# Attention and token/channel mixer on one core: batch 1's scores unpadded over 64 rows in two bursts, batch 0's output product by thirds of the weight

## The chip, the cores and the metric

The kernel runs on one core of a Trainium2 chip. The metric is the device time of one execution in microseconds (us). The kernel before was timed three times: 288.08, 288.24 and 288.31 us, median 288.24 us. The profile comes from a further execution of its own.

## The reference

Two parts follow each other. The first is windowed attention in 8 batches of 8 heads, 576 positions, head size 64: heads 0 to 3 see the last 32 positions ("plain"), heads 4 to 7 see every fourth of the last 128 ("dilated"). The second is a mixer over tokens, then over channels.

```
scores = scale * np.matmul(q, k.transpose(0, 1, 3, 2))          # scale = 1/8
mask_plain = (rel >= 0) & (rel < 32)                            # rel = query - key
mask_dil = (rel >= 0) & (rel < 128) & (rel % 4 == 0)
attn = softmax(np.where(mask, scores, -1e9)); x = attn @ v      # x: (8, 576, 512)
h = np.maximum(xt @ w_tok1, 0.0) @ w_tok2                       # 576 -> 256 -> 576
u = x + h.transpose(0, 2, 1)
h2 = np.maximum(u @ w_ch1, 0.0) @ w_ch2                         # 512 -> 1536 -> 512
return u + h2
```

## The kernel before, in words

**Stages.** A prelude does batch 0's attention and token mixing. Then one stage runs for each batch b. Its main part is `gen_main(b)`, the channel mixer: twelve products `gp` of four matmuls of 512 columns (L768), each with a relu into `gt`, then the output product `yp` (L787) for four blocks s of 128 tokens, 24 matmuls of 256 columns each, with u added by VectorE (L797) and a store. An odd batch carries the last 64 tokens of itself and of the batch before it (`gp_tails` L759, `yp` L807). A block of `gp` with mb from 8 to 11 reads the third piece of w_ch1 (`w_2` in the order, loaded at L860). The output product reads w_ch2 in three pieces of four mb each, loaded by the three DMAs at L988.

**What is woven in.** Between the matmuls of stage b stand steps for later batches: for batch b+1 the values `av` (L601 to L613), token mixing `h1p` (L625, L627), `up` (L637 to L650) giving u, and its transposes `tpu` (L664 to L675) giving `uT`; for batch b+2 casts of q, k and v to 16 bits, transposes `tp_q`, `tp_k`, `tp_t`, and scores. The function `interleave` merges the main part with lists of (time, cost, step), the times written by hand at the end of the file. It decides only the order in which the program is written; each engine then works strictly in that order and waits by semaphores. In the first stage (b = 0) both batch 1's scores and batch 2's are worked on, since the pipeline is filling.

**Scores.** Batches 0 and 1 use `scores_plain` and `scores_dil`: q lies padded with zeros over 128 rows (`qz`), and each score matmul (L425) is preceded by a "veil" (L423), a matmul of the identity with a table that puts −60000 where a key isn't seen. For a head pair that is, with veils, 12 matmuls of 160 columns, 4 of 128 and 8 of 64 if plain, 16 of 128 and 8 of 64 if dilated. After the veil no mask is needed. From batch 2 on (`twinned`) a burst `scores_twin(b, g)` does four heads at once (g = 0 plain, g = 1 dilated): the two heads of a pair use 64 rows each of TensorE, side by side (L510), 24 matmuls a burst, without veils. ScalarE takes the exponentials (L534) in the order of the last small pieces first for batch 2, and GpSimd multiplies by a 0/1 band afterwards (L112, on `attp`, `attt`, `attd`).

**Banks.** PSUM has three groups of banks: main (3, for gp and yp), sc (2) and fl (3, for transposes, av, h1p, up, tpu and part of a burst). A burst takes six banks: for batch 2 in the order fl, fl, sc, sc, fl, main. Who next wants a bank waits for its last reader.

**Queues.** Loads of q, k, v and the stores go out on SyncE's queue (SP); weights and many casts go through GpSimd (POOL). `gate` (L856) is a 1x1 copy on POOL that holds the loads of batch 2 back until the first piece of w_ch2 has landed. POOL's instructions stand in program order, so whatever waits there holds what is behind it.

Of the kernel before, what the change touches and what calls it, by code (L numbers as in the profile page):

```python
# [9 lines left out]
FP16 = mybir.dt.float16  # L10
FP32 = mybir.dt.float32
# [57 lines left out]
def kernel(  # L69
# [275 lines left out]
    def twinned(b):  # L345
        return b >= 2

# [150 lines left out]
    def scores_twin(b, g):  # L498

        tags = (("sc", 2), ("sc", 2), ("fl", 3), ("fl", 3), ("fl", 3), ("main", 3))  # L500
        if b == 2:
            tags = tags[2:4] + tags[0:2] + tags[4:6]
        ps = [bank(*tags[i], f"sc_{b}_{g}_{i}") for i in range(6)]
        small = ps[4:6]

        def twin(hp, banks, c, keys, queries):
            for h in range(2):
                rows = slice(64 * h, 64 * h + 64)
                n = c.stop - c.start
                nc.tensor.matmul(out=banks[h][:, c], lhsT=keys(rows), rhs=queries(rows), start=True, stop=True)  # L510

# [54 lines left out]

        def mask_tails():
            t = attt[:, 2 * g:2 * g + 2].rearrange("p a h c -> p (a h) c")[:, :, 64:TW].rearrange(
                "p z (x c) -> p z x c", c=128)[:, :, :, 0:64]
            mult(nc.gpsimd, t, t, tails_seen[g])  # L570

        yield from small_exps(1)
        if b == 2:
            yield from small_exps(0)
        for hp in (2 * g, 2 * g + 1):
            for h in range(2):
                main(hp, h)
                if h and (g or b == 2):
                    mask(hp)
                    if b == 2 and hp % 2 == 0:  # L580
                        mask_tails()
                yield 0.0
        if b > 2:
            yield from small_exps(0)
            if g == 0:
                mask(0)
            mask_tails()
            if g == 0:
                mask(1)
# [138 lines left out]

    def mix_steps(b, t_h1, t_h1b, t_u, t_uT, du=1.0, turn=6.0, gap=2.6):
        h1 = [sb.tile([128, DM], FP16, tag="h1", bufs=4, name=f"h1_{b}_{jb}") for jb in range(2)]  # L730
# [11 lines left out]
        else:  # L742
            for i, cb in enumerate(CBS):
                steps.append((t_uT + 0.9 * i, 0.28, lambda cb=cb: emit_uT(b, cb)))
        return steps

    def gen_main(b):
# [17 lines left out]
        for mb in range(NMB):  # L765
            p = bank("main", 3, f"gp_{b}_{mb}")
            for i, cb in enumerate(order):
                nc.tensor.matmul(out=p, lhsT=w3_block(cb, mb), rhs=uT[(b, cb)][0], start=(i == 0), stop=(i == 3))  # L768
                if i == 1:
                    yield 0.43  # L770
            relu(nc.vector if (mb % 2 == 1 if b == 0 else mb % 4 != 3 if b == 1 else mb in (1, 5)) else nc.scalar, gta[:, mb, m0:m0 + 512], p)
            yield 0.43
# [82 lines left out]
    def gate(t, src):  # L855
        nc.gpsimd.tensor_copy(out=t, in_=src)  # L856
# [127 lines left out]
    load_w3(2)  # L984
    for i in (2, 3, 4, 5, 7, 6, 8, 9, 10, 11):
# [5 lines left out]
    for cast in casts1[12:]:  # L991
        cast()

    new_qk(2)
    gate(l32[(2, "t")][0:1, 0, 0:1], w4[0][0:1, 0:1])
    for nm in ("q", "k"):
        load_tail(2, nm, nc.sync)
    for h0 in (0, 4):
        for nm in ("q", "k"):
            load_qk(2, nm, h0, h0 + 4, nc.sync)  # L1000
    load_v(2)

# [3 lines left out]
    for b in range(B):  # L1006
        steps = []
        if b == 0:
            steps += score_steps(1, 0, 0, (0.0, 0.7, 1.5),
                                 ((3.0, 5.2), (4.4, 7.0), (7.2, 9.6), (8.6, 11.4)))  # L1010
            va = value_steps(1, 13.4, 0.7)
            steps += va[:4] + [(p + 0.3, c, f) for p, c, f in va[4:]]
# [5 lines left out]
            steps += [(t, 0.25, f) for t, f in zip((25.2, 25.9, 27.0, 27.6, 28.2, 34.8, 35.2, 35.6, 36.0), bare)]  # L1018
            steps += scores2[:10]
            steps += at(34.0, 0.0, [lambda: emit_loads_qk(3)])  # L1020
        elif b == 1:
            va = value_steps(2, 0.0, 1.0)
            steps += [(0.8 + 0.4 * i, c, f) for i, (_, c, f) in enumerate(scores2[10:])]
            steps += [(t, c, f) for t, (_, c, f) in zip((2.2, 3.0, 4.8, 5.6, 8.2, 9.0, 10.4, 11.2), va)]
            steps += mix_steps(2, 7.0, 12.4, 14.6, 24.4, 1.0, 5.6, 0.8)
            casts = cast_steps(3)
            steps += [(6.0 + 0.5 * i, 0.0, casts[i]) for i in (0, 2, 4, 6, 8)]
            steps += [(9.5 + 1.0 * i, 0.0, lambda i=i: cast_qk(3, "q", i, nc.scalar)) for i in range(4)]
            steps += at(11.0, 0.3, casts[9:])
            steps += score_steps(3, 21.0, 4.6, lag=0.1)  # L1030
            steps += at(6.0, 0.0, [lambda: load_v(3)]) + at(20.8, 0.9, load_steps(4))
            steps += at(11.0, 0.9, dma_steps(3)) + at(17.0, 0.4, place_steps(3))
        else:
# [39 lines left out]
```

## Time and profile before

| | |
|---|---|
| median of three runs | 288.24 us |
| profiled execution, its own time | 289.66 us |
| its span in the trace | 287.8 us |
| TensorE (PE) busy in the span | 276.8 us |
| VectorE (DVE), ScalarE (ACT), GpSimd (POOL) busy | 132.1, 134.0, 163.0 us |
| first gp matmul of batch 0, first yp of batch 0 | 28.47, 50.38 us after the span's start |
| first gp matmul of batch 1, of batch 2 | 69.24, 105.06 us |

The profiled execution's own time is 1.86 us above its span (start and end outside the trace), and 1.42 us above the median of the other runs. A row of the timeline has the start in us, the duration in us, the engine, the line, the operation and "output<-inputs". A matmul's duration includes its way through the array; matmuls behind each other start closer together than they last, so the pitch, the distance of starts, is what one costs. A row of the windows view gives an interval, its length and each engine's busy time in it.

### The profile page before, as it was taken

How to read it: one execution, taken by the hardware profiler on the slowest of the kernel's cores; microseconds unless marked ns; L12 is line 12 of the kernel's file. 1: busy time of each engine (PE TensorE's matmuls, PEld its weight loads, DVE VectorE, ACT ScalarE, POOL GpSimd, SP SyncE). 2: the span in 40 equal slices, each digit the busy share in tenths (PEclk: the TensorE clock that was granted, in tenths of full speed). 3: DMA queues.
4: the chain of work that ended last, by engine and by line, in shares of the span. 5: the costliest groups of instructions: out<-in, count | busy, mean ns of one | idle time of the engine just before them, and what ended most of it. 6: DMA issues, size and time to landing. Idle time of an engine off the chain costs nothing.

```text
span 287.8 us, 6995 instructions
## 1 busy us (share of the span) xinstructions
PE 276.8 (96%) x2838; PEld 210.9 (73%) x2838; DVE 132.1 (46%) x278; ACT 134.0 (47%) x265; POOL 163.0 (57%) x221
## 2 busy tenths in 40 slices
PE   5879999999999999999999999999999999999995
PEld 2777676888766886698776976797766966886594
DVE  7747658446764236414640164416440274421022
ACT  2854673263543804574447615482546534225500
POOL 6961860478865799449970999279952930000000
PEclk9999999999999999999999999999999999999999
DMA  7999999993999998979888978299974210431023
GB/s 218 263 211 218 283 225 207 320 218 82 328 210 192 264 264 230 139 164 350 226 159 182 330 224 186 57 219 329 193 150 95 85 64 2 91 112 37 0 76 108
DMA packets 105551, 52.63 MB, mean 183 GB/s; under 512 B 73872, under 2 KB 104464, under 8 KB 105520
## 3 DMA queue, kind: packets, MB, share of 16 engines
q1 hardware_dynamic: 101280, 47.07, 67.0%
q0 software_dynamic: 2640, 3.94, 8.0%
q10 hardware_dynamic: 1600, 1.18, 1.4%
q8 instruction: 22, 0.36, 0.6%
q14 instruction: 9, 0.07, 0.1%
HBM read 37.07 MB, written 9.44 MB: 162 GB/s over the span
## 4 chain that ended last, share of the span: by engine, by line
PE 80%; DMA 8%; DVE 3%; POOL 3%; issue 2%; ACT 2%; ACTq 1%; SPq 0%; POOLq 0%; DVEq 0%
PE yp L787 29%; PE gp L768 24%; DMA l_vd<-in_v_dram 4%; PE h1p L627 4%; PE yp L807 3%; DMA l_k<-in_k_dram 3%; PE up L639 3%; PE sc L510 3%; PE gt L759 3%; DVE xn L112 1%; DMA kr<-c_k 1%; PE h1p L625 1%; PE av L608 1%; PE up L650 1%; PE av L603 1%
## 5 line engine op out<-in xcount | busy, mean ns | idle before, releaser
L787 PE MATMUL yp<-w,gt 128*128 128x256 f16 x756 | 87.1, 273 | 0.0
L787 PEld LDWEIGHTS <-gt 128*128 128x128 f16 x768 | 78.6, 106 | 6.5
L106 ACT ACTIVATE gt<-gp 128x512 f16<-128x512 f32 x69 | 41.2, 597 | 76.3 <-PE gp L768 76.0
L768 PE MATMUL gp<-utd,w 128*128 128x512 f16 x144 | 54.7, 380 | 0.0
L768 PE MATMUL gp<-utm,w 128*128 128x512 f16 x144 | 54.6, 379 | 0.0
L768 PEld LDWEIGHTS <-w 128*128 128x128 f16 x384 | 39.2, 114 | 20.3 <-issue 0.5
L797 DVE TENSOR_TENSOR o<-yp,u 128x512 f32<-128x512 f32 x31 | 21.4, 691 | 63.1 <-PE yp L787 58.5
L112 POOL TENSOR_TENSOR attp<-attp,const 128x1280 f16<-128x1280 f16 x12 | 31.4, 2616 | 27.5 <-ACT attp L534 27.4
L112 DVE TENSOR_TENSOR xn<-av,rec 128x320 f16<-128x320 f32 x64 | 31.4, 491 | 2.2
L112 POOL TENSOR_TENSOR attd<-attd,const 128x1024 f16<-128x1024 f16 x12 | 25.3, 2132 | 1.6 <-ACT attd L534 1.6
L768 PE MATMUL gp<-uT,w 128*128 128x512 f16 x96 | 25.8, 379 | 0.0
L108 DVE TENSOR_SCALAR gt<-gp 128x512 f16<-128x512 f32 x27 | 18.5, 686 | 13.6 <-PE gp L768 13.1
L645 DVE TENSOR_TENSOR u<-up,xn 128x512 f16<-128x512 f32 x26 | 17.9, 690 | 7.5 <-PE up L639 7.5
L534 ACT ACTIVATE attp<-sc 128x480 f16<-128x480 f32 (+1 forms) x36 | 16.1, 536 | 7.4 <-PE sc L510 7.4
L102 POOL CAST c_k<-l_k 128x512 f16<-128x512 f32 x29 | 18.0, 628 | 1.9 <-DMA l_k<-in_k_dram 1.7
L102 POOL CAST c_q<-l_q 128x512 f16<-128x512 f32 x27 | 16.8, 629 | 3.1 <-DMA l_q<-in_q_dram 3.1
L616 DVE RECIPROCAL rec<-av 128x5 f32<-128x5 f32 x64 | 12.2, 190 | 13.8 <-PE av L613 13.7
L106 ACT ACTIVATE h<-h1p 128x256 f16<-128x256 f32 x29 | 11.1, 384 | 14.5 <-PE h1p L627 14.1
L399 POOL COPY kt<-kr 128x512 f16<-128x512 f16 x10 | 10.7, 1075 | 9.0 <-DMA kr<-c_k 9.0
L697 ACT COPY utd<-utm 128x512 f16<-128x512 f16 x12 | 12.8, 1135 | 4.1 <-DMA utm<-u 4.1
L102 POOL CAST vv<-l_vn 128x256 f16<-128x256 f32 x32 | 12.0, 420 | 4.3 <-DMA l_vn<-in_v_dram 4.1
L112 POOL TENSOR_TENSOR attt<-attt,const 128x512 f16<-128x512 f16 x12 | 14.0, 1165 | 0.0
(147 smaller groups left out, 459.9 us busy)
## 6 DMA issues: line engine op xcount, KB each, us to landing
out_dram<-o SPq DMA_DIRECT2D x72, 128.0 KB, 3.1
l_q<-in_q_dram SPq DMA_DIRECT2D x15, 512.0 KB, 7.2
l_k<-in_k_dram SPq DMA_DIRECT2D x14, 512.0 KB, 7.1
l_vn<-in_v_dram SPq DMA_DIRECT2D x32, 128.0 KB, 6.6
l_vd<-in_v_dram SPq DMA_DIRECT2D x16, 256.0 KB, 4.6
w<-in_moe_w_ch_dram POOLq DMA_DIRECT2D x6, 512.0 KB, 7.6
lt<-in_q_dram SPq DMA_DIRECT2D x8, 128.0 KB, 4.6
l_vt<-in_v_dram SPq DMA_DIRECT2D x8, 128.0 KB, 4.9
```

Source lines behind the costliest of these rows:

```text
L102: eng.tensor_copy(out=out, in_=in_)
L106: nc.scalar.activation(out=out, in_=in_, func=AF.Relu)
L108: eng.tensor_scalar_max(out=out, in0=in_, scalar1=0.0)
L112: eng.tensor_tensor(out=out, in0=x, in1=y, op=ALU.mult)
L534: nc.scalar.activation(out=out, in_=in_, func=AF.Exp, scale=0.125)
L616: nc.vector.reciprocal(out=rec[:, :, 0], in_=av[:, :, 64])
L627: nc.tensor.matmul(out=p, lhsT=w[:, s, j], rhs=x[:, s, c], start=False, stop=(s == 3))
L645: nc.vector.tensor_tensor(out=u16(b, s), in0=blocks4(p), in1=blocks4(xn[b][:, s]), op=ALU.add)
L697: nc.scalar.copy(out=natural(uTd[:, cb - 2]), in_=uTm[i][:, cb].rearrange("p r m -> p m r"))
L768: nc.tensor.matmul(out=p, lhsT=w3_block(cb, mb), rhs=uT[(b, cb)][0], start=(i == 0), stop=(i == 3))
L787: nc.tensor.matmul(out=p[:, c], lhsT=gta[:, mb, a0:m0 + 512:4] if half else gta[:, mb, a0:a0 + 128], rhs=w4[mb][:, c], start=(mb == 0), st ...
L797: nc.vector.tensor_tensor(out=blocks4(o32), in0=blocks4(p), in1=u16(b, s), op=ALU.add)
```

## The change

Batch 1 joins the twinned batches. Its transposes become those of `bare_steps`, without padding, and its scores become two bursts. The plain heads' burst (g = 0) has no veils, and POOL multiplies `attp` and `attt` by the band, in two pairs of instructions. The dilated heads' burst (g = 1) keeps veils: 20 matmuls of 128 columns stand ahead of the 24 small ones, and no mask follows. Bursts of batch 1 use the bank order that batch 2 has. Values of batch 1 are taken dilated heads first: 4, 5, 6, 7, 0, 1, 2, 3.

Batch 0's output blocks 0, 1 and 2 are accumulated together in the three main banks, by thirds of w_ch2 (four mb at a time), block 3 afterwards as before. The first eight relus of batch 0's gp all go to DVE (before, every second one).

Casts of batch 1 move from POOL: the second half of q and two pieces of v to ACT, v's tail to DVE. The loads of batch 2 with their gate become a step of the stage, which on POOL stands between the two pairs of masks. The times of the lists of stages 0 and 1 are new: the second half of batch 2's transposes and its dilated burst go to stage 1, and batch 2's values, token mixing and batch 3's scores come 3 to 5 units later there.

```diff
     def twinned(b):
-        return b >= 2
+        return b >= 1
...
-        if b == 2:
+        if b <= 2:
             tags = tags[2:4] + tags[0:2] + tags[4:6]
...
+        veils = b == 1 and g == 1
...
+                nc.tensor.matmul(out=banks[h][:, c], lhsT=keys(rows), rhs=queries(rows),
+                                 start=not veils, stop=ends or not veils)
+        if veils:
+            for p in ps:
+                for r in range(4 if p not in small else 2):
+                    nc.tensor.matmul(
+                        out=p[:, 128 * r:128 * r + 128], lhsT=ident,
+                        rhs=veil[:, BLK + 128:BLK + 256] if p in small else veil[:, 0:128],
+                        start=(r == 0), stop=False)
...
-                if h and (g or b == 2):
+                if h and b == 1 and hp == 0:
+                    mask(0)
+                    mask_tails(0)
+                elif h and (b == 2 or (g and b > 2)):
                     mask(hp)
...
+        if b == 1 and g == 0:
+            mask(1)
+            mask_tails(1)
...
-            relu(nc.vector if (mb % 2 == 1 if b == 0 else ...
+            relu(nc.vector if (mb < 8 or mb % 2 == 1 if b == 0 else ...
...
+        if b == 0:
+            ps3 = [bank("main", 3, f"yp_{b}_{s}") for s in range(3)]
+            for i in range(3):
+                for s, p in enumerate(ps3):
+                    for half in range(2):
+                        c = slice(256 * half, 256 * half + 256)
+                        for mb in range(4 * i, 4 * i + 4):
+                            nc.tensor.matmul(out=p[:, c], ..., rhs=w4[mb][:, c],
+                                start=(mb == 0 and not half), stop=(mb == NMB - 1 and bool(half)))
+                        if half or i < 2:
+                            yield 0.43
...
-        for s in ((4, 0, 1, 2, 3) if odd else (0, 1, 2, 3)):
+        for s in ((4, 0, 1, 2, 3) if odd else (0, 1, 2, 3) if b else (3,)):
...
         if b == 0:
-            steps += score_steps(1, 0, 0, (0.0, 0.7, 1.5), ...
-            va = value_steps(1, 13.4, 0.7)
-            steps += mix_steps(1, 18.0, 20.6, 22.6, 31.4, 1.1)
+            bare = bare_steps(1)
+            steps += [(t, 0.25, f) for t, f in zip((2.8, 3.4, 5.0, 5.4, 6.0, 9.6, 10.2, 10.8, 11.4), bare)]
+            steps += score_steps(1, 7.2, 5.6, lag=0.25)
+            steps += [(6.2 + 0.6 * i, 0.0, lambda i=i: cast_qk(1, "q", 2 + i, nc.scalar)) for i in range(2)]
+            steps += at(9.0, 0.0, [loads2])
+            steps += [(14.6, 0.0, lambda: cast_tail_v(1, nc.vector))]
+            steps += [(15.0 + 0.5 * i, 0.0, lambda i=i: cast_vd(1, 2 * i, nc.scalar)) for i in range(2)]
...
+            steps += mix_steps(1, 23.4, 20.0, 25.6, 30.6, 1.0, gap_uT=0.8)
-            scores2 = score_steps(2, 29.6, 4.4, lag=0.25)
+            scores2 = score_steps(2, 34.0, 4.4, lag=0.25)
...
         elif b == 1:
-            steps += [(0.8 + 0.4 * i, c, f) for i, (_, c, f) in enumerate(scores2[10:])]
+            steps += [(0.4 + 0.4 * i, 0.25, f) for i, f in enumerate(bare[5:])]
+            steps += [(2.4 + 0.3 * i, c, f) for i, (_, c, f) in enumerate(scores2[10:])]
...
-            steps += score_steps(3, 21.0, 4.6, lag=0.1)
+            steps += score_steps(3, 25.4, 4.6, lag=0.1)
```

Three places of the order show what moves. The first is DVE at the border of stages 0 and 1. `o_0_s` is the sum that stores block s of batch 0; `uT_c` is batch 1's transposed u; `kt` and `kr` are batch 2's transposed k; `gt<-gp_m` is batch 1's relu; `u_1` is batch 1's u. Before:

```order
L797 TENSOR_TENSOR o_0_1_1100<-yp_1_1099,u_0_499 128x512
L102 COPY uT_0_1240<-tpu_0_1239 128x640
L102 COPY uT_3_1254<-tpu_3_1253 128x640
L797 TENSOR_TENSOR o_0_2_1215<-yp_2_1214,u_0_499 128x512
L102 COPY uT_1_1282<-tpu_1_1281 128x640
L387 COPY kr<-tp_k_2_1303 128x512
L388 COPY kt<-tp_k_2_1303 128x128
L387 COPY kr<-tp_k_3_1316 128x512
L388 COPY kt<-tp_k_3_1316 128x128
L797 TENSOR_TENSOR o_0_3_1296<-yp_3_1295,u_0_499 128x512
```

The same place after the change:

```order
L663 TENSOR_TENSOR u_1_1125<-up_3_1180,xn_628 128x4x128
L385 COPY kt<-tp_k_1_1186 128x512
L841 TENSOR_TENSOR o_0_3_1110<-yp_3_1109,u_0_499 128x512
L102 COPY uT_0_1216<-tpu_0_1215 128x640
L102 COPY uT_3_1224<-tpu_3_1223 128x640
L102 COPY uT_1_1232<-tpu_1_1231 128x640
L108 TENSOR_SCALAR gt<-gp_0_1293 128x512
L387 COPY kr<-tp_k_2_1305 128x512
L388 COPY kt<-tp_k_2_1305 128x128
L387 COPY kr<-tp_k_3_1318 128x512
L388 COPY kt<-tp_k_3_1318 128x128
L108 TENSOR_SCALAR gt<-gp_1_1325 128x512
```

The last sum of batch 0 stood behind the uT and the kr/kt copies; now it stands ahead of them, and the kr/kt copies lie between the first two relus of batch 1.

The second place is PE right behind batch 2's plain burst (`sc_0_i`). Before:

```order
L510 LDWEIGHTS kt
L510 MATMUL sc_0_5_1172<-tt,kt 128x64
L787 LDWEIGHTS gt
L787 MATMUL yp_1_1099<-w_87,gt 128x256
```

After:

```order
L512 LDWEIGHTS kt
L512 MATMUL sc_0_5_1244<-tt,kt 128x64
L786 LDWEIGHTS w_0_84
L786 MATMUL gp_0_1293<-uT_2_1199,w_0_84 128x512
L786 LDWEIGHTS w_0_84
L786 MATMUL gp_0_1293<-uT_0_1216,w_0_84 128x512
L378 LDWEIGHTS c_q_1092
L378 MATMUL tp_q_2_1296<-const,c_q_1092 128x128
```

Before, twelve matmuls of yp stood between the burst and the next transposes, which were those of batch 1's u (`tpu_2`); now two matmuls of batch 1's first gp stand there, ahead of transposes of batch 2's q.

The third place is POOL between the third piece of w_ch1 and the casts of batch 2 (`c_t`). `vv` and `vt` are v in 16 bits, `lt` the target of the gate. Before:

```order
L102 CAST c_q_611<-l_q_1_586 128x512 x2
L102 CAST c_k_614<-l_k_1_588 128x512 x2
L102 CAST vv_70<-l_vn_597 128x4x64 x3
L988 DMA w_87<-in_moe_w_ch_dram 128x2048 x3
L102 CAST vv_70<-l_vn_597 128x4x64
L102 CAST vv_70<-l_vt_600 64x8x64
L102 CAST vv_70<-l_vd_598 128x4x2x64 x2
L102 CAST vt_72<-l_vx_599 128x4x64
L856 CAST lt_637<-w_87 1x1
L102 CAST c_t_1067<-lt_637 128x512
```

After:

```order
L102 CAST c_k_614<-l_k_1_588 128x512 x2
L102 CAST vv_70<-l_vn_597 128x4x64 x3
L1032 DMA w_87<-in_moe_w_ch_dram 128x2048 x3
L102 CAST vv_70<-l_vn_597 128x4x64
L102 CAST vt_72<-l_vx_599 128x4x64
L112 ISA
L112 TENSOR_TENSOR attp<-attp,const 128x8x160
L112 TENSOR_TENSOR attt<-attt,const 128x2x2x64
L900 CAST lt_758<-w_87 1x1
L112 TENSOR_TENSOR attp<-attp,const 128x8x160
L112 TENSOR_TENSOR attt<-attt,const 128x2x2x64
L102 CAST c_t_1075<-lt_758 128x512
```

Five casts have left, four mask multiplies have come, and the gate, which releases the loads of batch 2 on SP, stands behind the first two of them.

More of the change, by code (lines that the diff above doesn't have):

```diff
@@ L743, in mix_steps @@
             for i, cb in enumerate(CBS):
-                steps.append((t_uT + 0.9 * i, 0.28, lambda cb=cb: emit_uT(b, cb)))
+                steps.append((t_uT + gap_uT * i, 0.28, lambda cb=cb: emit_uT(b, cb)))
         return steps
@@ L984 @@
     load_w3(2)
-    for i in (2, 3, 4, 5, 7, 6, 8, 9, 10, 11):
+    for i in (2, 3, 4, 6, 8, 9, 10, 11):
         casts1[i]()
```

66 lines of the change are left out of this document (41 added, 25 removed).

## The prediction

> **What bounds the kernel now.** I read the page's busy line first, then the windows of the stages that the change touches, then the chain that ended last.
>
> ```profile
> PE 276.8 (96%) x2838; PEld 210.9 (73%) x2838; DVE 132.1 (46%) x278; ACT 134.0 (47%) x265; POOL 163.0 (57%) x221
> 28.47:69.24 40.77, 40.11 (x462) 31.88 (x460) 24.67 (x54) 20.26 (x42) 24.43 (x42) 1.00 0.99 233
> 69.24:105.06 35.82, 35.22 (x376) 26.22 (x375) 17.59 (x35) 17.34 (x36) 26.81 (x27) 1.00 0.98 243
> 247.65 10.48 PE yp L787 x96
> 258.13 3.45 PE gp L768 x16
> ```
>
> PE works 96% of the span, and in the two stages touched 40.11 of 40.77 us and 35.22 of 35.82. So the time is PE's instruction stream: work taken from it is a gain, if nothing that it waits for comes later. The last two rows, of the chain, give prices without any wait: 10.48/96 = 0.109 us for 256 columns, 3.45/16 = 0.216 for 512. The time of a shape is this pitch, not the duration of a row.
>
> Busy time hides short waits, since a matmul is busy until its end leaves the array. So I counted the stream in the program's order between the first gp of batch 0 and the first of batch 2: over all 128 rows 112 matmuls of 512 columns, 268 of 256, 24 of 160, 180 of 128, 152 of 64 or 65; over 64 rows, at half a pitch each, 24 of 160, 40 of 128, 32 of 64. With these two pitches and those of the next fence that is 24.1 + 29.3 + 1.6 + 10.4 + 4.4 + 2.4 = 72.2 us of the 40.77 + 35.82 = 76.6 that passed. About 4.4 us are waits and edges.
>
> **What is saved.** Batch 1's scores, before, are 24 matmuls of 160 columns, 40 of 128 and 32 of 64, half of them veils. The pitches stand in the timeline of PE (four matmuls of 128, eight of 64, then four of 160 columns):
>
> ```profile
> 35.78 0.22 PE L423 MATMUL sm<-veil,const 128*128 128x128 f16 x1
> ...
> 36.01 0.19 PE L423 MATMUL sm<-veil,const 128*128 128x64 f16 x1
> ...
> 36.24 0.23 PE L423 MATMUL sc<-veil,const 128*128 128x160 f16 x1
> ...
> 36.45 0.23 PE L423 MATMUL sc<-veil,const 128*128 128x160 f16 x1
> ...
> 36.72 0.39 PE L309 MATMUL tp_q<-const,c_q 128*128 128x128 f16 x4
> ```
>
> That is 0.23/4 = 0.058, 0.23/8 = 0.029 and 0.27/4 = 0.068 us: 24 x 0.068 + 40 x 0.058 + 32 x 0.029 = 4.88 us. Batch 2's two bursts price the new form, edges included:
>
> ```profile
> 60.44 0.64 PE L510 MATMUL sc<-qt,kt 64*128 64x160 f16 x14
> ...
> 61.19 1.50 PE L787 MATMUL yp<-w,gt 128*128 128x256 f16 x12
> 62.65 0.38 PE L673 MATMUL tpu<-const,u 128*128 128x128 f16 x4
> 70.20 0.62 PE L510 MATMUL sc<-qt,kr 64*128 64x128 f16 x16
> ...
> 70.86 1.06 PE L768 MATMUL gp<-uT,w 128*128 128x512 f16 x4
> ```
>
> 61.19 - 60.44 = 0.75 and 70.86 - 70.20 = 0.66, and the dilated burst keeps 20 veils of 0.058 = 1.16: 2.57 us. Saved: 4.88 - 2.57 = **2.3 us**. The thirds of yp, the moved steps and the other order of values change no count of matmuls.
>
> **What is waited for instead.** I laid the pitches end to end in the new order from 28.47 on, and let each matmul start no sooner than what it reads. Eight places remain.
>
> (1) The ninth gp block. Ahead of it now stand 32 matmuls of 512 columns (6.9), 20 transposes (1.2) and one burst (0.75): PE is there at 37.3, with 0.4 for smaller waits on copies at 37.7. It reads the third piece of w_ch1:
>
> ```profile
> 30.76 0.77 POOL L860 DMA_DIRECT2D w<-in_moe_w_ch_dram  x1
> w<-in_moe_w_ch_dram POOLq DMA_DIRECT2D x1, 512.0 KB, 7.8
> 44.81 0.18 POOL L856 CAST lt<-w 1x1 f32<-1x1 f16 x1 [1.60 <-DMA w<-in_moe_w_ch_dram]
> ```
>
> 30.76 + 7.8 = 38.6, and nothing ahead of that DMA on POOL changes: a wait of 0.9 us (bounds 0.4 and 1.3). The third row is the gate, released when w_ch2's first piece landed: 44.8. The first third of yp gets there at 44.9, and the later thirds come after theirs by my walk, so w_ch2 costs nothing. Without thirds the first block would ask for all three pieces at once.
>
> (2) The copies for batch 1's bursts (k transposed on DVE): 0.45 us together, counted in part above.
>
> (3) Values of batch 1 start with a dilated head, and its v is now cast on ACT behind six exponentials. Prices:
>
> ```profile
> 57.93 0.60 ACT L643 CAST u<-up 128x512 f16<-128x512 f32 x1
> ...
> 61.93 0.39 ACT L534 ACTIVATE attp<-sc 128x256 f16<-128x256 f32 x1
> 62.19 0.40 ACT L534 ACTIVATE attt<-sc 128x256 f16<-128x256 f32 x1
> 62.46 1.53 ACT L534 ACTIVATE attp<-sc 128x480 f16<-128x480 f32 x3
> ```
>
> The burst ends at about 44.6; two small exponentials at a pitch of 0.27, four large ones at about 0.5 and a cast of 0.6 make 47.8, and PE would be there at about 47.0: 0.75 us (bounds 0 and 1.2).
>
> (4) The u blocks of batch 1 come closer together. u goes alternately through DVE and ACT (0.60 by the row above), three of them are waited for by the next `up` that takes their bank: 3 x 0.4 = 1.25 us (bounds 0.4 and 1.6).
>
> (5) The border of the stages. Prices on DVE:
>
> ```profile
> 64.06 0.49 DVE L102 COPY uT<-tpu 128x640 f16<-128x640 f16 x1 [1.29 <-PE tpu L667]
> 64.99 0.82 DVE L102 COPY uT<-tpu 128x640 f16<-128x640 f16 x1 [0.44 <-PE tpu L675]
> 65.73 0.68 DVE L797 TENSOR_TENSOR o<-yp,u 128x512 f32<-128x512 f32 x1
> 66.33 0.48 DVE L102 COPY uT<-tpu 128x640 f16<-128x640 f16 x1
> 67.03 0.42 DVE L387 COPY kr<-tp_k 128x512 f16<-128x512 f16 x1 [0.22 <-PE tp_k L378]
> 67.37 0.28 DVE L388 COPY kt<-tp_k 128x128 f16<-128x128 f16 x1
> ```
>
> Before, these copies ended by 66.8, and 18 yp matmuls still covered them. Now the last sum of batch 0 (0.68) and three copies (0.49, 0.82, 0.48) follow each other on DVE, 2.5 us, with batch 2's plain burst behind them, since it takes fl banks that the copies read. Some 1.2 us of transposes and pieces of yp lie beside them: 1.3 us are left (bounds 0.6 and 2.0).
>
> (6) Directly behind the burst stand two gp matmuls (0.43) and then transposes of q into a bank that ACT frees with its fourth exponential. The rows above show the same release: burst over at 61.19, fourth exponential over at 62.19 + 0.40 = 62.59, next transpose at 62.65, so 1.4 us, which twelve yp matmuls (1.31) covered. Two gp matmuls leave 1.0 us.
>
> (7) The k transposes that follow need a bank that DVE frees behind a gp relu, a kr and a kt copy (about 0.69, the price of the sum, plus 0.42 and 0.28): 1.0 us (bounds 0 and 1.4).
>
> (8) Token mixing waits for short ones, 0.4 us.
>
> Sum: 0.9 + 0.45 + 0.75 + 1.25 + 1.3 + 1.0 + 1.0 + 0.4 = 7.05, and 0.4 for edges that stay as they are: 7.45 us against 4.4 before, **+3.05**.
>
> **The next stage.** POOL gets batch 2's and 3's work later:
>
> ```profile
> 95.19 2.62 POOL L112 TENSOR_TENSOR attp<-attp,const 128x1280 f16<-128x1280 f16 x1 [2.69 <-ACT attp L534]
> ...
> 105.59 1.20 POOL L112 TENSOR_TENSOR attt<-attt,const 128x512 f16<-128x512 f16 x1
> ```
>
> Batch 3's masks begin with the first row and end with the second, 11.6 us later, in one piece. Before, their first burst was written some 14 us ahead of the first gp of batch 2, now some 10, and the first values stand right behind that gp. By the walk the last mask is 0.8 us late, but the head that needs it is the fifth of eight, and POOL's start depends on what SP's queue brings; I take half, **+0.4** (bounds 0 and 1.2). Later stages are as before: SP's transposes by DMA pace them, and PE's stream is the same.
>
> For batch 1 itself POOL is in time: its first mask starts at about 43, mask, tail, gate, mask and tail end by 49.4, and the first plain values come at 50.3. The gate passes at 46.2 instead of 44.8; the loads of batch 2 behind it on SP move by 1.4 us, and the step that reads them has moved further.
>
> **The sum.** -2.3 + 3.05 + 0.4 = +1.15. The profiled execution took 289.66 us (span 287.8 and 1.86 around it), the median is 288.24; a difference holds for both, so I forecast 288.24 + 1.15 = **289.4 us**. With all terms at their better ends it would be 4.2 us less, 285.2, at their worse ones 3.1 more, 292.5. They don't all fall on one side: the distances added as squares give 1.8 down and 1.3 up, so its own range is 287.6 to 290.7.
>
> **Rivals.**
>
> *The covers hold* (faster). The walk stacks waits that may overlap: whoever has waited at (1) and (3) comes later to (4) to (7), and transposes or gp matmuls that I put behind a wait could stand ahead of it by a few hundred ns. For it speaks that before, in the same crowded stretch, only 4.4 us were lost; against it, that (6) and (7) follow from the order and a measured release. If (3) to (7) come to half, 2.65 instead of 5.3, and the next stage to nothing, it is 288.24 + 1.15 - 2.65 - 0.4 = 286.3; with a wait or two of them whole, 287.0. It decides from 1.75 us less waiting than I count.
>
> *No change.* Waits just eat up the saving: 288.2. It takes a total 1.15 lower than mine.
>
> *The shared port* (slower still). POOL now multiplies for some 5 us in one go while DVE casts v's tail for batch 1, which before it did at the start:
>
> ```profile
> 11.76 0.45 DVE L102 CAST c_k<-l_k 128x512 f16<-128x512 f32 x1
> 10.75 1.17 POOL L102 CAST c_q<-l_q 128x512 f16<-128x512 f32 x2
> ```
>
> Such a DVE cast began here while POOL cast up to 11.92, and took 0.45 us, so at most 0.16 of it can be blocking. Were it blocked through a whole mask of 2.62 us, the tail would be ready at about 49.2 and the first values' last matmul 1.25 us later than I have it: 290.7. The Trainium skill ("SBUF — State Buffer", section "SBUF: two separate sides") has it that a DVE operation in its two-port mode and a GpSimd operation hold the shared ports exclusively and the loser is blocked entirely; by that rule the block could last a whole mask, and the row neither shows nor excludes it, since POOL had only 0.16 us left.
>
> *The change doesn't do what it says*: halves of a pair in batch 1 run one after the other. The accumulated veils could bring that about, since they use all 128 rows. Both bursts would cost about 1.2 us more: 290.6. Batch 2's rows speak against it; taken together with the port rival.
>
> **Chances.** Forecast 0.50; covers hold 0.31; no change 0.10; the two slower rivals 0.09. A measurement can tell about 0.2% from no change, 0.58 us: between 287.7 and 288.8 counts as the same, which takes the no-change case and a little of the forecast and of the covers. Faster 0.31, same 0.15, slower 0.54. The range, 286.7 to 291.2, leaves out the better part of the first rival and what lies beyond the worse ends.
>
> **What would show it.** In the profile after: gp's first matmul of batch 1 at about 68.5 (69.24 before) and that of batch 2 at about 105.8 (105.06). The ninth gp block starts at 38.6, released by a DMA. Between the plain burst of batch 2 and the next q transposes lie about 1.4 us. The release of (7) shows as idle time of PE ahead of `tp_k`. I am wrong if the first gp of batch 2 comes before 104.5: then the waits of (4) to (7) were covered, and the values' rows and the idle column of PE will say which. If it comes at 105.8 and the end still isn't later, the slack was in the stages after. If the first value of batch 1 stands at 49, it was the port.

## The result, and the profile after

The change makes the kernel slower: 292.08 us median (291.90 to 293.46, four runs) against 288.27 (288.08 to 288.36), a ratio of 1.0143 with a 95% interval of 1.0118 to 1.0167. Forecast were 289.4 us, +1.15, with a range up to 291.2. The sign was right, the size is more than three times as large.

The page's busy line, and the windows of stages 0 and 1 (from the first gp matmul of a batch to that of the next), for the changed kernel, first profile:

```profile
PE 277.0 (95%) x2810; PEld 209.3 (72%) x2810; DVE 134.2 (46%) x277; ACT 134.3 (46%) x267; POOL 166.5 (57%) x220
26.65:70.09 43.44, 38.56 (x417) 28.97 (x415) 25.59 (x50) 16.54 (x34) 23.97 (x38) 0.96 0.97 232
70.09:108.17 38.08, 36.34 (x395) 27.18 (x391) 18.21 (x38) 21.22 (x46) 27.16 (x27) 1.00 0.81 190
```

The stages took 40.77 and 35.82 us before; now they take 43.44 and 38.08, although 45 matmuls fewer are recorded in the first (417 against 462; the second has 19 more, 395 against 376, since part of batch 2's scores moved there). PE was busy for all but 0.66 us of stage 0 before; now it stands for 4.9 us. From batch 3's first gp on both kernels are alike to 0.1 us a stage.

One profile is one execution. The first gp stood at 28.47 us before and at 26.65 here, with a prelude that wasn't touched, so I took both kernels' profiles again (windows of stages 0, 1 and 2; before first, then the changed kernel):

```profile
27.94:68.70 40.76, 40.11 (x461) 31.84 (x459) 24.66 (x54) 20.24 (x42) 23.82 (x42) 1.00 0.98 232
68.70:104.14 35.44, 35.05 (x376) 26.22 (x375) 17.57 (x35) 17.31 (x36) 27.43 (x28) 1.00 1.02 246
104.14:132.84 28.70, 28.70 (x292) 21.96 (x291) 12.71 (x27) 15.11 (x30) 20.79 (x28) 1.00 0.91 207
```

```profile
27.25:69.27 42.02, 37.38 (x417) 28.59 (x414) 27.02 (x50) 16.53 (x34) 23.68 (x38) 1.00 0.98 232
69.27:107.36 38.09, 36.36 (x395) 27.19 (x391) 18.21 (x38) 21.21 (x46) 27.17 (x27) 1.00 0.79 183
107.36:137.35 29.99, 29.04 (x293) 22.00 (x292) 12.72 (x27) 15.09 (x30) 24.45 (x30) 1.00 1.02 238
```

The second pair gives the account: +1.26 in stage 0, +2.65 in stage 1, +1.29 in stage 2, -0.69 in the prelude (which differs from one execution to the next): +4.5 us, as the times of these two executions do (293.19 against 288.74). These two differ by more than the medians, 3.6 to 3.8 us; 293.19 is the slowest of its four. The first pair adds up otherwise: +2.67, +2.26, +0.74 and -1.82 in the prelude are +3.85, and the times, 293.46 against 289.66, differ by 3.80. So the parts of the loss vary from one execution to the next more than their sum does.

Where PE stands in stage 0 is seen in the timeline of PE of the first profile, around the ninth gp block:

```profile
35.10 1.06 PE L786 MATMUL gp<-uT,w 128*128 128x512 f16 x4
38.70 1.90 PE L786 MATMUL gp<-uT,w 128*128 128x512 f16 x4 [2.54 <-DMA w<-in_moe_w_ch_dram]
40.38 0.63 PE L378 MATMUL tp_q<-const,c_q 128*128 128x128 f16 x4
40.81 0.94 PE L786 MATMUL gp<-uT,w 128*128 128x512 f16 x2
41.59 0.39 PE L378 MATMUL tp_k<-const,c_k 128*128 128x128 f16 x4
```

PE is 9.3 us behind its first gp when it needs the third piece of w_ch1 (35.10 and four pitches, 35.96; the forecast had 9.2), and waits 2.54 us for it. What follows is slow: four matmuls of 512 columns take 1.68 us from start to start, not 0.86. The windows view has the reason in its column of the granted clock, 0.52 for 2.89 us:

```profile
38.70:41.59 2.89, 2.89 (x11) 1.33 (x12) 0.00 (x0) 0.96 (x2) 2.36 (x5) 0.52 0.88 159
41.59:44.30 2.71, 2.56 (x22) 1.56 (x21) 1.81 (x5) 0.94 (x3) 1.49 (x2) 1.00 1.02 204
```

That is 1.4 us of the first profile's 293.46 us; the other three runs of it, at a whole clock, took 291.90 to 292.11. In the second profile the wait is 1.33 us and the clock stays at 1.

The border of the stages, timeline of PE, first profile:

```profile
70.09 0.62 PE L786 MATMUL gp<-uT,w 128*128 128x512 f16 x2
71.53 0.38 PE L378 MATMUL tp_q<-const,c_q 128*128 128x128 f16 x4 [0.82 <-ACT attt L545]
71.75 0.59 PE L786 MATMUL gp<-uT,w 128*128 128x512 f16 x2
72.18 0.39 PE L378 MATMUL tp_k<-const,c_k 128*128 128x128 f16 x4
72.46 0.38 PE L378 MATMUL tp_q<-const,c_q 128*128 128x128 f16 x4
73.75 0.38 PE L378 MATMUL tp_k<-const,c_k 128*128 128x128 f16 x4 [0.91 <-DVE kt L388]
```

From 70.09 to 71.53 are 1.44 us for two matmuls that cost 0.43: the 1.0 us of term (6). From 72.46 to 73.75 are 1.29 for 0.22, 1.07 lost: the 1.0 of term (7). Both stand where the prediction put them.

### The profile page after: what moved, and what is told of

It is laid out like the page before. It is cut to its first block, busy times and chain, and to the rows that moved or that the text cites. A ratio compares the mean times of both kernels' runs of the same rounds, so it can differ in the third digit from the quotient of the medians.

```text
span 291.7 us, 6941 instructions
## 1 busy us (share of the span) xinstructions
PE 277.0 (95%) x2810; PEld 209.3 (72%) x2810; DVE 134.2 (46%) x277; ACT 134.3 (46%) x267; POOL 166.5 (57%) x220
## 4 chain that ended last, share of the span: by engine, by line
PE 81%; DMA 9%; POOL 3%; ACT 2%; DVE 2%; issue 1%; SPq 0%; POOLq 0%; ACTq 0%
PE gp L786 25%; PE yp L831 24%; PE h1p L645 4%; PE up L657 4%; DMA l_q<-in_q_dram 4%; PE gt L777 4%; PE yp L851 4%; DMA w<-in_moe_w_ch_dram 3%; PE sc L512 3%; DMA l_k<-in_k_dram 2%; PE yp L810 2%; PE h1p L643 1%; PE av L626 1%; PE av L621 1%; PE up L668 1%
## 5 line engine op out<-in xcount | busy, mean ns | idle before, releaser
L831 PE MATMUL yp<-w,gt 128*128 128x256 f16 x684 | 77.9, 273 | 0.0
L831 PEld LDWEIGHTS <-gt 128*128 128x128 f16 x696 | 71.3, 106 | 6.3 <-issue 0.6
L106 ACT ACTIVATE gt<-gp 128x512 f16<-128x512 f32 x65 | 38.9, 598 | 67.0 <-PE gp L786 66.7
L112 POOL TENSOR_TENSOR attp<-attp,const 128x1280 f16<-128x1280 f16 x14 | 36.6, 2612 | 36.8 <-ACT attp L545 36.8
L841 DVE TENSOR_TENSOR o<-yp,u 128x512 f32<-128x512 f32 x28 | 19.4, 692 | 60.3 <-PE yp L831 50.9
L108 DVE TENSOR_SCALAR gt<-gp 128x512 f16<-128x512 f32 x31 | 21.3, 688 | 16.6 <-PE gp L786 15.9
L545 ACT ACTIVATE attp<-sc 128x480 f16<-128x480 f32 (+1 forms) x42 | 18.7, 537 | 14.7 <-PE sc L512 14.7
L102 POOL CAST c_q<-l_q 128x512 f16<-128x512 f32 x25 | 15.6, 627 | 3.8 <-DMA l_q<-in_q_dram 3.8
L112 POOL TENSOR_TENSOR attt<-attt,const 128x512 f16<-128x512 f16 (+1 forms) x14 | 15.4, 1102 | 0.0
L545 ACT ACTIVATE attt<-sc 128x256 f16<-128x256 f32 x28 | 11.2, 402 | 7.7 <-PE sc L512 7.7
```

The lines of the kernel that those rows point to most:

```text
L102: eng.tensor_copy(out=out, in_=in_)
L106: nc.scalar.activation(out=out, in_=in_, func=AF.Relu)
L108: eng.tensor_scalar_max(out=out, in0=in_, scalar1=0.0)
L112: eng.tensor_tensor(out=out, in0=x, in1=y, op=ALU.mult)
L545: nc.scalar.activation(out=out, in_=in_, func=AF.Exp, scale=0.125)
L831: nc.tensor.matmul(out=p[:, c], lhsT=gta[:, mb, a0:m0 + 512:4] if half else gta[:, mb, a0:a0 + 128], rhs=w4[mb][:, c], start=(mb == 0), st ...
```

## The experiments

Theory A is the prediction's: separate waits, each of which goes when its cause goes. Theory B: up to the output product of batch 0 the transfers set the pace, and work saved on PE there only becomes waiting for them. Theory C is the rival of the shared port. All kernels were compared with runs of the kernel before on the same chip; there its median lay between 288.4 and 288.8 us, its runs between 287.6 and 290.4. The second profiles of both kernels were expected thus:

> The kernel before, unchanged, for a second profile. The first one had its first gp matmul at 28.47 us, the changed kernel's profiles so far at 26.4 to 27.3, with a prelude that the change does not touch. If the prelude is the same in both, it comes at about 27 here and the span is about 1.4 us below 287.8; if the change had made the prelude faster, at 28.5.

> The changed kernel, unchanged, for a second profile. The first one held a wait of 2.54 us for w_ch1's third piece and a granted clock that fell behind it; other kernels with the same first stage waited 1.0 to 1.6 us. Expected: 1.0 to 2.5 us of wait here, the clock whole if it is below 2 us, and 3 to 4 us above the kernel before.

Measured: first gp at 27.94 us, 288.32 us (ratio to its own other runs 0.9991, 0.9976 to 1.0006); the changed kernel 291.93 us, ratio 1.0119 (1.0089 to 1.0149). In the profiles of the kernel before and its variants the first gp stands between 26.66 and 28.47, in those of the changed kernel and its variants between 26.41 and 27.89: the ranges overlap, so that an earlier prelude is not shown to come from the change. The difference of the medians is 3.6 us, 3.8 in the first comparison.

**The third piece of w_ch1, earlier.** In the changed kernel:

```diff
+    load_w3(2)
     new_qk(1)
     gate(l32[(1, "t")]...
...
-    load_w3(2)
```

> The changed kernel, with the load of the third piece of w_ch1 issued about 9 us earlier on POOL, ahead of the gate of batch 1's loads. Theory A (single waits): the 2.54 us that PE waits ahead of the ninth gp block go, and nothing of that size comes in their place: about 289.6 us against 292.1. Theory B (the transfers set the pace): the DMA engines are busy 97 to 99% of this stretch, so 512 KB put ahead only push batch 1's q, k and v back by about 2.2 us; PE waits for the transposes instead: 291.5 to 292.5.

Measured: 292.9 us (291.29 to 295.29), ratio 1.0166 (1.0114 to 1.0219). The wait is gone, and others have come, as the waits of PE from 27.3 to 50 show:

```profile
PE tp_q L378 <- POOL c_q L102: 0.8, 2, 0.6
PE av L626 <- ACT vv L100: 0.5, 1, 0.5
PE tp_k L378 <- POOL c_k L102: 0.5, 1, 0.5
PE tp_t L368 <- POOL c_t L102: 0.5, 1, 0.5
```

Batch 1's q and k are cast later, since their loads come later. Theory B; the four runs spread over 4 us, so that all they show is that nothing was won.

**Fewer bytes.** Both kernels without the loads of batch 1's v, whose casts then read batch 0's:

```diff
-    load_v(1)
+    for part in ("vn", "vd", "vx", "vt"):
+        l32[(1, part)] = l32[(0, part)]
```

> The changed kernel without the loads of batch 1's v (its casts read batch 0's v; 1.25 MB less of loads). Theory B (the transfers set the pace of the first 46 us): w_ch1's third piece lands early enough, the wait ahead of the ninth gp block goes, and 1.0 to 2.5 us are won: 289.6 to 291. Theory A, order alone: the wait for it is one latency of the queue and stays near 1 us, and nothing is won beyond 0.5 us.

> The kernel before without the loads of batch 1's v, as above. Theory B: here 48 more matmuls stand ahead of the ninth gp block and cover the landing, so taking the transfers away wins nothing, 288.0 to 288.6; what the changed kernel wins by it and this one does not is what the transfers cost the change. Rival: both win alike, and the transfers are no part of the difference.

Measured: the changed kernel 290.55 us (290.34 to 291.01), 1.4 below the changed kernel's second median, ratio to before 1.0063 (1.0045 to 1.0081), with no wait of gp for a DMA left; the kernel before 289.14 us, ratio 1.0015 (0.9998 to 1.0032), nothing won. In the kernel before the padded scores covered the landing of the weight: in its first profile the piece lands at 38.6 and PE comes to the ninth gp block at 44.1. So up to 1.4 us of the change's cost are work taken from under a transfer; up to, since DVE's cast of v (below) also ran clear of PE's need in this profile.

**The border.** In the changed kernel the second half of batch 2's transposes and its dilated burst come later:

```diff
-            steps += [(0.4 + 0.4 * i, 0.25, f) for i, f in enumerate(bare[5:])]
-            steps += [(2.4 + 0.3 * i, c, f) for i, (_, c, f) in enumerate(scores2[10:])]
+            steps += [(1.7 + 0.45 * i, 0.25, f) for i, f in enumerate(bare[5:])]
+            steps += [(4.2 + 0.3 * i, c, f) for i, (_, c, f) in enumerate(scores2[10:])]
```

> The changed kernel, with the second half of batch 2's transposes written some 1.3 units later in stage 1 and its dilated burst 1.8 later, so that four more gp matmuls pairs lie between the plain burst and the transposes. Theory A: the waits for the banks that ACT and DVE free (1.01 and 1.07 us in the profile) go: 290.0 to 290.4 us. Theory B: what follows on the values and masks comes later by as much: 292 us.

Measured: 290.77 us, ratio 1.0079 (1.0050 to 1.0109), so 1.2 us below the second run of the changed kernel. In its profile stage 1 took 36.47 us instead of 38.08, and of the two waits one of 0.3 us is left. Theory A, with 1.6 of the 2.1 us in the stage; the median lies between the values expected of A and of B.

**No thirds.** The output product of batch 0 by whole blocks:

```diff
-        if b == 0:
+        if False:
             ps3 = ...
-        for s in ((4, 0, 1, 2, 3) if odd else (0, 1, 2, 3) if b else (3,)):
+        for s in ((4, 0, 1, 2, 3) if odd else (0, 1, 2, 3)):
```

> The changed kernel with batch 0's output product by whole blocks as before, so that the first block needs all of w_ch2. The last piece lands at about 50.3 in the changed profile, PE comes to the product at 46.6. Theory A and B: it waits some 3 us more, 294 to 295 us. Rival: the steps woven in between cover it, and the thirds are worth nothing: 292 us.

Measured: 295.11 us, ratio 1.0242 (1.0204 to 1.0280), 3 us above the changed kernel. Waits of PE from 40 to 60 us:

```profile
PE yp L831 <- DMA w<-in_moe_w_ch_dram: 3.6, 2, 2.4
```

The thirds do what they look like: they keep the product from waiting for all of w_ch2. Some of the 3 us are the clock's: all four executions ran at a mean granted clock of 0.988 to 0.994.

**Batch 3's scores as early as before.**

```diff
-            steps += score_steps(3, 25.4, 4.6, lag=0.1)
+            steps += score_steps(3, 21.0, 4.6, lag=0.1)
```

> The changed kernel with batch 3's scores at 21.0 in stage 1 as before, instead of 25.4. Theory A: the 0.6 to 0.7 us that stage 2's values wait for POOL's last mask go: 291.4 us. Rival: POOL is then still at batch 2's masks and casts, or the burst waits for its k, and nothing is won: 292.1 us or above.

Measured: 299.15 us, ratio 1.0345 (1.0300 to 1.0390). In its profile, of the slowest execution (302.94 us, 13.7 us of it at a granted clock of 0.50), PE's bursts wait 3.0 us for POOL's `kt` copies, which aren't there yet, against the 0.6 that the edit was after. The rival: the later place in the list follows from what was pushed into stage 1.

**The casts of batch 1's v.** All three on ACT, ahead of the exponentials:

```diff
-            steps += [(14.6, 0.0, lambda: cast_tail_v(1, nc.vector))]
-            steps += [(15.0 + 0.5 * i, 0.0, lambda i=i: cast_vd(1, 2 * i, nc.scalar)) for i in range(2)]
+            steps += [(12.4, 0.0, lambda: cast_tail_v(1, nc.scalar))]
+            steps += [(12.4, 0.0, lambda i=i: cast_vd(1, 2 * i, nc.scalar)) for i in range(2)]
```

What it answers to stands in the second profile of the changed kernel, one fence each for DVE, POOL and PE:

```profile
45.49 3.41 DVE L102 CAST vv<-l_vt 64x512 f16<-64x512 f32 x1
```

```profile
44.65 0.66 POOL L112 TENSOR_TENSOR attt<-attt,const 128x256 f16<-128x256 f16 x1
45.26 0.18 POOL L900 CAST lt<-w 1x1 f32<-1x1 f16 x1
45.40 2.60 POOL L112 TENSOR_TENSOR attp<-attp,const 128x1280 f16<-128x1280 f16 x1
47.96 0.65 POOL L112 TENSOR_TENSOR attt<-attt,const 128x256 f16<-128x256 f16 x1
```

```profile
47.67 0.28 PE L626 MATMUL av<-vv,attd 128*128 128x65 f16 x4 [0.57 <-ACT vv L100]
47.79 0.19 PE L629 MATMUL av<-vt,attt 128*128 128x65 f16 x1
48.96 0.19 PE L631 MATMUL av<-vv,attt 128*128 128x65 f16 x1 [0.98 <-DVE vv L102]
```

A cast that took 0.42 us in the prelude takes 3.41: it began 0.09 us after POOL's second mask and ended at 48.90, when both multiplies were over (48.61). PE then waits 0.98 us for it.

> The changed kernel with the three casts of batch 1's v (tail from DVE, two pieces from behind the exponentials) put on ACT ahead of the dilated burst's exponentials, where ACT stood idle for 1.7 us. In the last profile of the changed kernel DVE's cast took 3.41 us beside POOL's masks, and PE waited 1.0 us for it and 0.6 for ACT's casts. Theory C (the shared port): both waits go, in most executions: 290.3 us, 1.6 below the changed kernel. Rival: the cast was late for another reason, its load; then ACT waits for it as DVE did and the exponentials behind it come later: 292 us or above.

Measured: 290.67 us (290.02 to 292.07), ratio 1.0083 (1.0051 to 1.0116): 1.3 us below the changed kernel, though the intervals of the two ratios overlap. Both waits are gone; from batch 0's output product to batch 1's first gp it is 22.72 us, against 24.58 in the second and 23.46 in the first profile.

**The tail's cast alone.** Still on DVE, ahead of the masks:

```diff
-            steps += [(14.6, 0.0, lambda: cast_tail_v(1, nc.vector))]
+            steps += [(11.6, 0.0, lambda: cast_tail_v(1, nc.vector))]
```

> The changed kernel with nothing moved but the cast of batch 1's v tail: still on DVE, but written 3 units earlier, ahead of POOL's masks. Theory C (DVE's cast is blocked while a mask runs): it takes about 0.4 us again, the wait of up to 1.1 us of the first values goes in those executions that have it, and the median is 291.0 to 291.5; ACT's casts still cost 0.6 to 0.7. Rival (the load of the tail was late): the cast waits for its load now, and the median stays at 291.9 or rises.

Measured: 292.08 us, but from 290.65 to 294.42, ratio 1.0122 (1.0078 to 1.0166). In its profile the cast takes 0.41 us and PE's wait for it is gone; the median doesn't show it. The clock hides it at least in part: four of the six executions had a mean granted clock of 0.992 to 0.994 and took 291.55 to 294.42, the two at 0.998 and 1.000 took 290.88 and 290.65, and two are too few to show a gain. In the profile, one of the four, the clock is at 0.50 at the border of the stages (windows view):

```profile
68.87:72.29 3.42, 2.87 (x20) 1.80 (x18) 1.43 (x4) 2.71 (x6) 2.62 (x2) 0.50 0.89 289
```

The wait isn't in every execution, either: of six profiles with the cast at its place in the changed kernel, it took 0.42 and 0.50 us where it began just ahead of the second mask, 1.98 to 3.50 in the other four, and PE waited about 1 us for it in two.

**The blocking by itself.** The kernel before with casts strewn over stage 3:

```diff
+    def probe(i):
+        if i % 2 == 0:
+            nc.vector.tensor_copy(out=p16, in_=p32)
+        else:
+            nc.scalar.copy(out=p16b, in_=p32[:, 0:128])
...
+            if b == 3:
+                steps += [(2.0 + 0.6 * i, 0.0, lambda i=i: probe(i)) for i in range(48)]
```

> The kernel before with 24 casts on DVE (128x256, 32 to 16 bits, between scratch tiles in SBUF) and 24 on ACT (128x128) strewn over stage 3, where POOL masks batch 5; they add nothing to the output. Theory C: a DVE cast that starts beside one of POOL's multiplies lasts as long as what is left of that multiply, up to 2.6 us, instead of about 0.25 us, and ACT's casts always last the same. Rival (bandwidth shared): all DVE casts beside a mask are longer by the same small factor, below 2.

Measured: minimum, median and maximum of the 24 casts on DVE and of the 24 on ACT, in ns, from the views of these two lines:

```profile
L1010 DVE CAST probe<-probe x24: 275/582/2691, 135.6 to 166.4; 128x256 f16<-128x256 f32 x24
```

```profile
L1012 ACT CAST probe16b<-probe x24: 289/291/366, 134.1 to 165.1; 128x128 f16<-128x128 f32 x24
```

And beside POOL's masks (timelines of DVE and POOL):

```profile
157.11 3.34 DVE L1010 CAST probe<-probe 128x256 f16<-128x256 f32 x3
160.37 0.68 DVE L797 TENSOR_TENSOR o<-yp,u 128x512 f32<-128x512 f32 x1
160.97 3.26 DVE L1010 CAST probe<-probe 128x256 f16<-128x256 f32 x2
164.15 0.68 DVE L797 TENSOR_TENSOR o<-yp,u 128x512 f32<-128x512 f32 x1
```

```profile
157.68 2.62 POOL L112 TENSOR_TENSOR attp<-attp,const 128x1280 f16<-128x1280 f16 x1 [6.15 <-ACT attp L534]
160.25 1.21 POOL L112 TENSOR_TENSOR attt<-attt,const 128x512 f16<-128x512 f16 x1
161.42 2.66 POOL L112 TENSOR_TENSOR attp<-attp,const 128x1280 f16<-128x1280 f16 x1
```

A row here merges casts that follow each other. Of the first three, two ran ahead of the mask; the third, the 2.69 us of the view, began at 157.75, just behind the mask's start, and ended 0.15 after the mask's end at 160.30. Of the next two the second ended at 164.23, 0.15 after the next mask's end at 164.08. It isn't a matter of multiplies alone: a cast on DVE that began at 137.10, beside a cast on POOL that ended at 137.58, took 0.63 us, until 137.73. The sum `o<-yp,u`, which reads PSUM, takes its usual 0.68 beside the masks, and ACT's casts never change. Theory C, as an effect; that the two engines share a port is not seen in a trace, only that one waits for the whole of the other's instruction. The rule cited in the prediction (the Trainium skill, "SBUF — State Buffer", section "SBUF: two separate sides") says that whichever of the two starts later is blocked entirely, and these rows bear it out for DVE's casts.

**Veils for the plain heads too, no masks.** 20 veil matmuls more, in the plain burst (`veils = b == 1`, masks of batch 1 left out, the veil's columns in the burst's order).

> The changed kernel with veils for batch 1's plain heads as well, 12 matmuls of 160 columns and 8 of 128 more (1.3 us of PE), and no masks on POOL. If POOL's masks cost PE nothing: 1.3 us slower, 293.2. Theory C: DVE's cast isn't blocked (+1.0 back), and POOL, free of 6.5 us of masks, brings batch 2's and 3's casts and masks earlier (0.4 to 0.7 back in stage 2): 291.9, the same.

Measured: 293.62 us (292.78 to 296.07), ratio 1.0194 (1.0152 to 1.0235). Without masks on POOL, DVE's cast of the tail takes 0.41 us at the place where it took up to 3.50 beside them, which is theory C once more. POOL's masks are worth having, 1.5 us or more against the veils; and without them stage 2 still takes 17.31 us to its output product (17.30 and 17.31 in the changed kernel's two profiles), so POOL's masks of batch 1 aren't what delays the masks of batch 3.

**Together.** The later border, the casts on ACT and, in stage 2, the dilated heads' values 0.9 later:

```diff
-                steps += value_steps(b + 1, 0.4, 0.95) + mix_steps(...)
+                va = value_steps(b + 1, 0.4, 0.95)
+                steps += va[:4] + [(t + 0.9 * (b == 2), c, f) for t, c, f in va[4:]] + mix_steps(...)
```

> The later border of stage 1, the casts of v on ACT, and in stage 2 the dilated heads' values 0.9 later, together. Theory A, each wait adds up: 291.9 - 1.6 (border) - 1.6 (casts) - 0.6 (last mask) = 288.1, even with the kernel before. If waits only move, 289.5 or above.

Measured: 289.23 us (288.05 to 291.31), ratio 1.0027 (1.0003 to 1.0050). 2.7 us of the 3.6 are won back. Then the same with w_ch1's third piece one cast earlier (`casts1[0]()`, `load_w3(2)`, then the others):

> The same with the third piece of w_ch1 issued one cast earlier on POOL, at about 28.7 instead of 29.9, while POOL would wait for q's load. Theory A: up to 1.2 us of the 1.0 to 1.3 us of wait goes: 287.1, below the kernel before. Theory B (transfers set the pace): what lands earlier pushes the others, as when it was put ahead of all loads: 288.1 or above.

Measured: 289.44 us (288.24 to 292.19), ratio 1.0036 (1.0003 to 1.0070). Nothing won. The profile is of an execution near the upper end (291.87). In it the wait for w_ch1's piece is still 1.2 us, and PE stands another 1.73 us ahead of the first yp, until 47.02. The view names ACT's exponentials, but the DMAs of w_ch2 tell better (the row of their issue on POOL, then from the view of that line the time to landing):

```profile
39.88 1.61 POOL L1031 DMA_DIRECT2D w<-in_moe_w_ch_dram  x3
```

```profile
DMA to landing us min/median/max: 7.1/9.2/11.8
```

39.88 + 7.1 = 47.0. They are issued 1.9 us later than in the combination without this edit (38.01), behind casts of v that wait for their loads. But 1.3 of the 1.9 lie in the prelude of this execution (first gp at 27.84, against 26.57), so that only some 0.6 can be the edit's. Theory B by the median; the profile alone doesn't show it.

Last, with the tail on DVE ahead of the masks, and batch 1's `tp_q_2` and `tp_k_2` moved into the wait (times 9.6 and 10.2 become 8.4 and 8.5):

> The combination of the later border, ACT's two casts ahead of the exponentials and stage 2's later values, now with the v tail cast on DVE ahead of the masks, and eight transposes of batch 1 moved into the wait ahead of the ninth gp block. Theory A: 0.4 to 0.9 us of that wait (1.3) is used: 288.4 to 288.8, level with the kernel before. Theory B: the landing moves nothing else, so that much is won; if transposes there wait for their banks instead, 289.2 or above.

Measured: 289.01 us (288.48 to 289.86), ratio 1.0017 (0.9999 to 1.0035): level with the kernel before within the interval. The wait for the weight is gone, and the transposes wait in its place (PE, 27 to 50 us):

```profile
PE tp_q L378 <- ACT attt L545: 0.8, 1, 0.8
PE tp_k L378 <- ACT qt L383: 0.7, 1, 0.7
```

No version tried beats the kernel before.

## Why the forecast was wrong in size

The ledger was the right kind of sum, and most of its terms held. In the second profile, by starts less pitches (the idle column is shorter, since a matmul counts as busy to its end): (2) 0.45, measured 0.49; (3) 0.75, measured 0.73; (5) 1.3, measured 0.50 + 0.70; (6) 1.0 and 1.0; (7) 1.0 and 1.1. Rows of PE that stand behind waits, for (4), (5) and the next stage:

```profile
59.28 0.38 PE L668 MATMUL up<-h,w 128*128 128x512 f16 x1 [0.30 <-DVE h L108]
61.64 0.38 PE L657 MATMUL up<-h,w 128*128 128x256 f16 x2 [0.23 <-ACT u L661]
64.22 0.38 PE L657 MATMUL up<-h,w 128*128 128x256 f16 x2 [0.23 <-ACT u L661]
67.81 0.23 PE L512 MATMUL sc<-qt,kt 64*128 64x160 f16 x1 [0.34 <-DVE uT L102]
68.54 0.63 PE L512 MATMUL sc<-qt,kt 64*128 64x160 f16 x13 [0.50 <-DVE uT L102]
112.77 0.20 PE L629 MATMUL av<-vt,attt 128*128 128x65 f16 x1 [0.57 <-POOL attt L112]
126.18 0.44 PE L512 MATMUL sc<-qt,kt 64*128 64x160 f16 x8 [0.38 <-POOL kt L399]
```

Term (4) counted three waits for the banks of u, 1.25 us. Two came, of 0.39 each, released by ACT. The first row's 0.46 is a wait of token mixing for its relu, so it belongs to term (8), with 0.4 more in shorter waits of token mixing: 1.64 together against 1.65, so the sum of the two terms held and the split didn't. The first third of yp came within the landing of w_ch2, and the thirds are worth 3 us. These steps failed:

- *Term (1), 0.9 us.* It set the landing of the piece, 38.6, against PE's arrival, 37.7, and counted the arrival from one execution's first gp, 28.47. The distance was right, 9.2 forecast and 9.3 measured; the starting point was not. In eight profiles with this order of stage 0 (the changed kernel's two and six of its variants) the first gp stands at 26.4 to 27.3, PE needs the piece at 35.8 to 36.6, and it lands at 37.3 to 38.7. By starts less pitches that is a wait of 1.1 to 2.7 us, 2.7 and 1.5 in the two profiles of the changed kernel. Behind the 2.7 the clock fell as well, for 1.4 us more, which no row of the kernel before could show. The prediction took the DMA for one late transfer. Issued earlier, it only moved the wait to batch 1's casts (292.9 us); with fewer bytes to load, up to 1.4 us were won. So PE ran into the transfers of the whole stage, which kept the DMA engines at a share of 0.97 to 0.99.
- *The rival of the port, chance under 0.09 and no term in the sum.* It was worked out to 1.25 us and measured at 1.1 in the second profile; in the first the cast took 1.98 us and PE didn't wait for it. The sign given for it, a first value of batch 1 at 49, misled: the first value stands at 49.63 in the profile without that wait, whose output product began late, and at 47.67 in the one with it. The row that I set against it had only 0.16 us of overlap, so it could bear neither way, and I should have carried it as an unknown with both ends. The casts together, term (3)'s among them, cost 1.3 us at the median.
- *The next stage, 0.4 us.* Half was taken of one wait of 0.8. The wait was there, 0.73, and in some executions a second one, PE's burst for POOL's `kt`, 0.58 in the second profile: 1.3 us together there, against 0.74 in the first profile's stage. Taking half of a wait that the walk gave was a choice without a row.
- *Edges left as they were, 0.4 us.* Between the two first gps, 27.25 to 107.36, the second profile lost 80.1 - 69.9 = 10.2 us, where 7.45 were forecast: 1.7 of the rest are the first two points above, about 1 us lies in places of below 0.35 each that I had not listed. The kernel before lost 4.0 in its second profile, not 4.4, and 2.7 of these 4.0 lay in places of below 0.35 each. In the changed kernel such places make 2.6: the small waits stayed, and the ledger, which listed the long ones, had 0.4 for them beside the short terms (2) and (8).

Summed: 1.15 + 2.75 + 0.4 + 0.9 - 0.7 for the prelude is 4.5, the difference of the second profiles (0.7 to 0.9 more than that of the medians). The saving of 2.3 us itself was never in doubt: the bursts run side by side and no product was added. What is left after the combinations, 0.5 to 0.8 us, I can't put down to one cause: the saved work is spent on the chain from u to batch 1's first gp (terms (4) and (5)) and on the wait for the weight, which moved when it was filled.

## What to carry to other kernels

Before counting work off the bound engine as a gain, look at the DMA share of the stage: where it is near 1 (0.97 to 0.99 here), ask for each transfer what covered it so far, since it may land when it did, and the saved work becomes a wait. When long waits are listed against the total that the kernel lost before, list the short ones too: they stay. When an operation changes its engine, look at what the other engine does at that time, not only at whether it is free. And where a forecast sets two times from different parts of the program against each other, take their spread from more than one execution.

## What the runs showed of the hardware

A cast on DVE from SBUF to SBUF (32 to 16 bits) that starts beside an instruction on POOL that also works from SBUF to SBUF doesn't end before that instruction does: beside masks 0.28 us became up to 2.69, and in the rows of the strewn casts the end came 0.15 us behind the mask's. DVE's sums that read PSUM (0.68 us) and ACT's casts (0.29 at the median) were not touched.

The granted clock of TensorE fell to 0.52 for 2.9 us behind a wait of 2.5 us for a DMA, and stayed at 1 behind one of 1.3. It doesn't take one long wait: in the profile with the tail's cast moved alone it was at 0.50 for 3.42 us at the border of the stages, where no wait was longer than 1.0 us, and in the changed kernel's second profile the same border, with the same waits, passed at a clock of 1. Why one execution fell and the other didn't is not shown.
